# VectorE's share of a softmax: steps one by one with three buffers each, checks grouped by four sets, a plan priced by issue intervals, and 117 key tiles shared out by set

## The chip, the cores and the metric

The kernel runs on one core of a Trainium2 chip. The metric is the device time of one execution in microseconds (us). The engines are TensorE (PE in the profile, its weight loads PEld), VectorE (DVE), ScalarE (ACT), GpSimd (POOL) and SyncE (SP, here a queue that issues DMAs).

## The reference

Two attention layers on the same input x (2048 rows, 512 columns, bf16, 32 heads of 16), mixed by a gate g for each row:

```python
g = sigmoid((x * gate_w).sum(-1, keepdims=True))
# A: linear attention with a learned feature map
phi = concat([softmax(q_or_k @ w_phi), softmax(-(q_or_k @ w_phi))])   # 32 features a head
a = (phi_q @ (phi_k^T @ v)) / (phi_q @ phi_k.sum(rows) + 1e-6) @ A_wo
# B: ordinary attention
b = softmax(q @ k^T * 16**-0.5) @ v @ B_wo
out = g * a + (1 - g) * b
```

Layer B holds nearly all of the work: 32 heads x 2048 x 2048 scores, each of which needs an exponential.

## The kernel before, in words

**Sets and key tiles.** Layer B is cut into 32 sets. A set is one chunk of 512 queries (`qc`, four), one group of eight heads (`g`, four) and one half of that group (`par`, two): four heads. Each set goes over 16 key tiles (`kt`) of 128 keys. For a key tile and a set there are 4 heads x 512 queries of scores, made by TensorE (L745) in two pairs of 128x1024 scores, each in one of three slots of PSUM (`R_r`).

**Two ways to the exponential.** For most key tiles ScalarE takes the exponential of a pair from PSUM (L764, tile E in SBUF, a ring of eight buffers; the first ones lie in memory that layer A uses later, with the names phiK and vA). For `NDVE[n]` of the 16 key tiles of set n, 109 over all sets, VectorE makes the exponential from integer arithmetic: two conversions from PSUM to int16 (L754, named `di` in the plan) into a tile I, a mask step from I to F (L770, `dm`), a product of I and F into F (L773, `dw`), and a mask step on I (L777, `de`). All these tiles are named D in the profile. The products with the values are then made from F and from I (L787) where ScalarE's tiles need one such product (L800): four matmuls each, all added up in one PSUM bank, O, of which there is one. When a set's products are done, O is copied to SBUF (L464, tile OT), transposed (L825), divided by its sum (L829, L836), and its reciprocals go through a check on GpSimd (L831, L833, L835). The checks guard the shortcut without a maximum in the softmax: a verdict at the end (L899 to L904) would start a slow exact path, which doesn't run with these inputs.

**Wide packs.** `WIDE` is 2: VectorE's key tiles of a set are taken in packs of two where there are two, and L770 and L777 then take both in one instruction of 4096 elements. The memory for it is three wide tiles, two for I (`I_r`) and one for F (`F_r`).

**Projections and layer A.** In between run the projections of K and Q for the groups (L470; the copies L492 and L464), in one further PSUM bank (`M_r`), the projection of V, layer A's feature maps (ScalarE L627, VectorE L629 and L633, GpSimd's product L634) and its small products, and the output projection (L876, L884, L889, L892, DMAs at L894). A Q block, but for the first, is copied to `qs` and then spread over zeroed tiles `q` by eight DMAs on SP's queue (L514). The first one is masked by four VectorE steps instead (L505). GpSimd sets the other three q tiles to zero (L441).

**The order.** A planner in the kernel's own Python (`_Sched`) sets the order of each engine's instructions ahead of time. Every operation has a price in us, a due time (`prio`, mostly from `ut(u)`, where 32 units are one set) and buffers; the planner places operations one after the other by those prices. On the chip only the order is left: each engine goes through its list, and waits for semaphores where an operation needs another's result or buffer. `KLEAD`, `KLEAD1` and `QLEAD` say how many units ahead of its set a K or Q block is due, `RUSH_K` how many us earlier than due it may push in on TensorE, `LEAD` how far VectorE's tiles run ahead, `FULL` at how many occupied E buffers products that free one are put first, and `SLACK` and `LAT` are waits that the plan adds after an operation.

Of the kernel before, what the change touches and what calls it, by code (L numbers as in the profile page):

```python
# [7 lines left out]
F32 = mybir.dt.float32  # L8
# [26 lines left out]
NDVE = [0, 1] + [4, 3, 4, 4, 3] * 6  # L35
LEAD = 6.0
EXTRA = 1.2
WIDE = 2
FULL = 9
SLACK = 0.8  # L40

LAT = 0.06
STAY = 1.0
PAIRS = (0, 1, 2, 3, 4, 5, 6, 7)
RUSH = 1.0
# [3 lines left out]
RUSH_O = 30.0  # L49
VLEAD = 3.0  # L50
KLEAD1 = 24
KLEAD = 56
QLEAD = 24
EARLY = 10.0
# [23 lines left out]
class _Op:  # L78
    __slots__ = ("eng", "fn", "dur", "prio", "deps", "tiles", "mode", "name", "dma",
                 "n_open", "users", "after", "late", "start", "end", "count", "sem", "vc", "seq", "est", "parts", "feeds", "frees")  # L80


class _Sched:
# [9 lines left out]
    def add(self, eng, prio, dur, fn, deps=(), tiles=(), mode=None, name="", dma=None, nb=0.0, after=(), parts=1, feeds=None):  # L93
# [5 lines left out]
        o.mode, o.name, o.dma, o.est = mode, name, dma, nb  # L99
        o.frees = any(t.slots is self.stock for t in tiles)  # L100
# [8 lines left out]
    def next_pe(self, cands, first, last_mode):  # L109
# [5 lines left out]
        def rank(w, o):  # L115
            if o.feeds == "act" and pending("act", w) < (3 if last_mode == "row" else 2):
                return 0
            if short and o.frees:
                return 0.5
            if o.feeds == "dve" and pending("dve", w) < 1:  # L120
                return 1
            return 2
# [17 lines left out]
    def run(self):  # L140
# [16 lines left out]
        left = len(self.ops)  # L157

        def slot_time(t):
            best = None  # L160
            for i, ten in enumerate(t.slots.tenant):
                if ten is None:
                    when = 0.0
                elif any(x.end is None for x in ten.ops):
                    continue
                else:
                    when = max(x.end for x in ten.ops) + LAT
# [4 lines left out]
        def earliest(o, at):  # L172
            when = max(at, o.est)
            for t in o.tiles:
# [7 lines left out]
        while left:  # L182
# [16 lines left out]
            if pick is None:  # L199
                seen = set()  # L200
                for o in self.ops:
                    for t in o.tiles:
                        if id(t) not in seen and t.idx is not None and any(x.end is None for x in t.ops):
                            seen.add(id(t))
                            print("held", [(x.name, x.end, x.n_open) for x in t.ops][:8], str(t.slots.aps[0])[:60])
# [18 lines left out]
            o.end = w + dur + (o.dma or 0.0) + (0.17 if o.eng == "pe" else 0.0)  # L224
# [10 lines left out]
            for u in o.users:  # L235
                u.n_open -= 1
                late = u.late if o.end > 60 and u.eng == "pe" and o.eng in ("dve", "pool") else 0.0
                u.est = max(u.est, o.end + LAT + late)
# [85 lines left out]
def _build(ctx, nc, A_x, A_wqkv, A_w_phi, A_wo, B_wqkv, B_wo, gate_w, out):  # L324
# [39 lines left out]
    E_r = ring(8, [128, 1024], name="E")  # L364
    D_wide = [sb([128, 4096], I16, name="D")[:] for _ in range(3)]
    D_all = [d[:, 2048 * i:2048 * (i + 1)] for d in D_wide for i in range(2)]
    sch.stock = E_r
    I_r, F_r = _Slots(D_wide[0:2]), _Slots(D_wide[2:3])
    watv = WAT[:].rearrange("p a b -> p (a b)")
    eA_r = _Slots([watv[:, 1024 * i:1024 * (i + 1)] for i in range(4)])  # L370
    acc = sb([128, 136], F32, name="acc")
# [10 lines left out]
    rB_r = ring(3, [128, 4, 4], F32, name="rB")  # L382
# [15 lines left out]
    ez = acc[:, 80:96]  # L398
# [50 lines left out]
    MM = 0.235  # L449
    tset = [T0]  # L450
    for n in NDVE:
        tset.append(tset[-1] + 2 * (NT - n) * 0.935 + EXTRA)

# [7 lines left out]
    def evac(eng, prio, dst, src, deps, tiles, n=512, name="ev"):  # L461
        if eng == "act":
            return add("act", prio, 0.1 + n * 0.00084, lambda e: e.copy(dst(), src()), deps=deps, tiles=tiles, name=name)
        return add("dve", prio, 0.14 + n * 0.00105, lambda e: e.tensor_copy(dst(), src()), deps=deps, tiles=tiles, name=name)  # L464
# [18 lines left out]
    def k_proj(g, c, prio, tile, off, eng="dve"):  # L483
        f = fill(prio, tile, off, lambda t: W_Bk[:, t, 128 * g:128 * (g + 1)],
                 lambda t: xT[:, t, NQ * c:NQ * (c + 1)], op_x[c] + [op_wk1 if g else op_wk0], f"kf{g}{c}", RUSH_K)
        use_wk.append(f)
        dst, src = (lambda: kT[:, g, NQ * c:NQ * (c + 1)]), (lambda: tile.ap[:, off:off + 512])
        if eng == "act":
            ev_k[g, c] = add("act", prio, 0.53, lambda e: e.activation(dst(), src(), ACTF.Copy, scale=KFAC),
                             deps=[f], tiles=[tile], name=f"kev{g}{c}")  # L490
        else:
            ev_k[g, c] = add("dve", prio - RUSH_K, 0.68, lambda e: e.tensor_single_scalar(dst(), src(), KFAC, ALU.mult),  # L492
                             deps=[f], tiles=[tile], name=f"kev{g}{c}")

    def q_proj(g, c, prio, tile, off):

        f = fill(prio, tile, off, lambda t: W_Bq[:, t, 128 * g:128 * (g + 1)],
                 lambda t: xT[:, t, NQ * c:NQ * (c + 1)], op_x[c] + [op_wq1 if g else op_wq0], f"qf{g}{c}", RUSH_K)
        qt = q_t[g, c] = _Tile(q_r)
        if (g, c) == (0, 0):  # L500
# [7 lines left out]
            ev_q[g, c] = ms  # L508
            return
# [28 lines left out]
    for t in range(KT):  # L538

        def fn(e, t=t):  # L540
            ins = None
            for i in range(4):
                ins = e.transpose(txv()[:, t, 128 * i:128 * (i + 1)], xs[:, i, 128 * t:128 * (t + 1)], ident[:])
            return ins
        xtp.append(add("pe", -80 + t, 0.35, fn, deps=[op_x0, op_id], tiles=[tx], mode="full", name="xtp"))
    op_x[0] = [add("act", -80, 0.94, lambda e: e.copy(xT[:, 0:2, 0:NQ], txv()[:, 0:2, :]), deps=xtp[0:2], tiles=[tx], name="xev"),
               add("dve", -80, 0.69, lambda e: e.tensor_copy(xT[:, 2:4, 0:NQ], txv()[:, 2:4, :]), deps=xtp[2:4], tiles=[tx], name="xev")]  # L547
# [18 lines left out]
    for g in range(1, KT):  # L566
# [5 lines left out]
        q_proj(g, 0, ut(64 * g - QLEAD), t, 0)  # L572
# [8 lines left out]
    for part in range(4):  # L581
# [7 lines left out]
        gops.append(add("pe", ut(64), 0.5, gate_mm, deps=sum(op_x, []) + op_gw, tiles=[tg], mode="full", name="gate", nb=ut(60)))  # L589
# [8 lines left out]
    for w in range(2):  # L598
        for t in range(KT):
            tile = _Tile(M_r)  # L600
            prio = ut(66 + 4 * (4 * w + t))
# [7 lines left out]
            f = add("pe", prio, 0.35, fn, deps=[op_wat] + op_wbd, tiles=[tile], mode="full", name="wp", nb=prio - EARLY)  # L609
# [4 lines left out]
    accA, accB, okB, tmpB = acc[:, 0:64], acc[:, 64:80], acc[:, 96:112], acc[:, 112:128]  # L614
    op_acc0 = pool(-94.5, 0.2, lambda e: e.memset(acc[:, 0:80], 0.0), nb=LATER)
    op_acc = pool(-94.4, 0.2, lambda e: e.memset(acc[:, 96:112], 1.0), [op_acc0], nb=LATER)

    def phi(prio, w, st, dst, dst_deps, dst_tiles):
# [8 lines left out]
        o5 = [add("act", prio + 1, 0.58, lambda e, a=a: e.activation(ev()[:, :, a, :], P(), ACTF.Exp, scale=1.0 - 2.0 * a),  # L627
# [457 lines left out]
```

## Time and profile before

| | us |
|---|---|
| median of 3 runs (830.16 to 833.79) | 832.17 |
| the profiled execution, its own time | 833.28 |
| its span (first to last instruction) | 831.5 |
| ScalarE busy in the span | 782.4 (94%) |
| VectorE busy | 688.2 (83%) |
| TensorE busy, modelled ends | 745.2 (90%) |
| GpSimd busy | 149.3 (18%) |
| granted TensorE clock, mean | 0.982 |

In the lines of the profile a group is a source line, an engine and an operation with its tiles, then busy time and the mean of one in ns, then the idle time of the engine before them and what ended it. Durations on VectorE and ScalarE include the end of an instruction, over which the next one already starts: two that follow each other without a pause overlap by about 0.08 us on VectorE and 0.2 us on ScalarE. So the price of an instruction in a row of them is the time from its start to the next one's start, which the timeline shows. Windows give the busy time of each engine in a stretch of the span.

### The profile page before, as it was taken

To read this page: it belongs to the slowest core of one execution; us is meant where nothing else is said; L and a number is where in the kernel's file an instruction comes from. 1 tells how busy PE (TensorE), PEld (TensorE's weight loads), DVE (VectorE), ACT (ScalarE), POOL (GpSimd) and SP (SyncE) were. 2 spreads that over 40 slices of the span, in tenths; PEclk is the share of its full clock that TensorE was granted. 3 is DMA by queue.
4 is the path that set the end of the run, shared out by engine and by line. 5 is a ranking of instruction groups with operands and counts; after the bars stand their busy time and mean duration, and the time that the engine had idled before them with its cause. 6 is when DMAs were issued, how large, how long until landed. Compare 5 with 4: busy or idle time off the path is not lost.

```text
span 831.5 us, 13591 instructions
## 1 busy us (share of the span) xinstructions
PE 745.2 (90%) x5684; PEld 228.4 (27%) x5684; DVE 688.2 (83%) x747; ACT 782.4 (94%) x881; POOL 149.3 (18%) x195
## 2 busy tenths in 40 slices
PE   7999999989989999897798999989988999888886
PEld 2223232222222222232222222223222222222222
DVE  3255898889998999989989879899888988798891
ACT  3969999989999999999999899999999999899995
POOL 7000002212232323101032201120013111130000
PEclk9999999999999999999999999999999999899999
DMA  9100000100000000000202101111012110111000
GB/s 220 34 8 2 7 7 1 7 8 1 14 1 13 1 7 8 13 13 14 62 20 41 26 20 25 28 32 32 14 32 20 39 26 13 39 26 26 8 1 28
DMA packets 55922, 19.56 MB, mean 24 GB/s; under 512 B 48304, under 2 KB 55856, under 8 KB 55856
## 3 DMA queue, kind: packets, MB, share of 16 engines
q1 hardware_dynamic: 52960, 17.06, 9.6%
q10 hardware_dynamic: 2640, 1.57, 0.8%
q8 instruction: 46, 0.75, 0.4%
q14 instruction: 20, 0.16, 0.1%
q0 software_dynamic: 256, 0.02, 0.0%
HBM read 3.69 MB, written 2.10 MB: 7 GB/s over the span
## 4 chain that ended last, share of the span: by engine, by line
ACT 59%; PE 20%; DVE 17%; SPq 2%; issue 1%; DMA 1%; DVEq 0%
ACT E L764 54%; PE ps L745 8%; DVE D L754 4%; PE ps L470 4%; DVE D L773 4%; PE ps L800 3%; SPq L514 2%; DVE D L770 2%; ACT WAT L627 2%; PE ps L787 2%; ACT phiK L764 2%; PE ps L876 2%; DVE ss L629 2%; DVE D L777 1%; ACT vA L764 1%
## 5 line engine op out<-in xcount | busy, mean ns | idle before, releaser
L764 ACT ACTIVATE E<-ps 128x1024 bf16<-128x1024 f32 x782 | 728.9, 1144 | 27.1 <-PE ps L745 19.8
L745 PE MATMUL ps<-q,kT 64*128 64x512 bf16 x2048 | 372.8, 390 | 69.9 <-ACT E L764 43.0
L754 DVE TENSOR_SCALAR D<-ps 128x1024 int16<-128x1024 f32 x218 | 264.9, 1215 | 64.3 <-PE ps L745 63.6
L745 PEld LDWEIGHTS ps<-q,kT 64*128 64x128 bf16 x2048 | 92.0, 93 | 306.0 <-ACT E L764 217.7
L800 PE MATMUL ps<-E,vB 128*32 128x512 bf16 x1564 | 154.7, 396 | 2.3 <-ACT E L764 0.8
L773 DVE TENSOR_TENSOR D<-D 128x2048 bf16<-128x2048 bf16 x109 | 138.8, 1292 | 0.5
L787 PE MATMUL ps<-D,vB 128*32 128x512 bf16 x872 | 83.3, 398 | 0.6 <-DVE D L773 0.6
L770 DVE TENSOR_SCALAR D<-D 128x4096 int16<-128x4096 int16 (+1 forms) x61 | 70.3, 1153 | 7.1 <-PE ps L787 6.0
L777 DVE TENSOR_SCALAR D<-D 128x4096 int16<-128x4096 int16 (+1 forms) x61 | 73.5, 1205 | 0.2
L631 POOL TENSOR_TENSOR acc<-acc,ss 128x64 f32<-128x64 f32 x32 | 21.0, 656 | 286.3 <-DVE ss L629 286.3
L831 POOL TENSOR_TENSOR acc<-acc,rB 128x16 f32<-128x16 f32 x32 | 18.0, 563 | 289.5 <-DVE rB L829 289.5
L800 PEld LDWEIGHTS ps<-E,vB 128*32 128x32 bf16 x1564 | 38.6, 93 | 92.6 <-issue 79.9
L470 PE MATMUL ps<-Wp,xT 128*128 128x512 bf16 x128 | 49.7, 394 | 0.1
L470 PE MATMUL ps<-xT,WB 128*128 128x512 bf16 x128 | 48.1, 391 | 1.8 <-DVE xT L547 0.8
L629 DVE TENSOR_REDUCE ss<-WAT 128x64 f32<-128x1024 bf16 x32 | 38.8, 1211 | 2.1 <-ACT WAT L627 2.0
L634 POOL TENSOR_TENSOR WB<-WAT,ss 128x1024 bf16<-128x1024 bf16 x16 | 37.9, 2370 | 12.8 <-DVE ss L633 12.7
L627 ACT ACTIVATE WAT<-ps 128x512 bf16<-128x512 f32 x64 | 38.0, 701 | 0.8 <-PE ps L470 0.8
L634 POOL TENSOR_TENSOR phiK<-WAT,ss 128x1024 bf16<-128x1024 bf16 x16 | 34.6, 2163 | 16.7 <-DVE ss L633 16.7
L825 PE MATMUL ps<-ident,OT 128*128 128x128 f32 x128 | 33.9, 315 | 0.6 <-DVE Wp L892 0.3
L787 PEld LDWEIGHTS ps<-D,vB 128*32 128x32 bf16 x872 | 21.2, 95 | 38.0 <-issue 32.6
L876 PE MATMUL ps<-phiK 128*128 128x512 bf16 x88 | 30.4, 386 | 0.2 <-ACT E L764 0.2
L464 DVE CAST vB<-ps 128x1024 bf16<-128x1024 f32 x8 | 9.8, 1224 | 23.2 <-PE ps L470 23.2
(98 smaller groups left out, 375.8 us busy)
## 6 DMA issues: line engine op xcount, KB each, us to landing
out_dram<-Wp SPq DMA_DIRECT2D x16, 128.0 KB, 1.7
q<-qs SPq DMA_DIRECT2D x120, 16.0 KB, 1.8
WB<-in_B_wqkv_dram ACTq DMA_DIRECT2D x2, 384.0 KB, 11.0
D<-in_A_x_dram SPq DMA_DIRECT2D x1, 512.0 KB, 4.6
WB<-in_B_wqkv_dram ACTq DMA_DIRECT2D x1, 512.0 KB, 9.6
WAv<-in_A_wqkv_dram SPq DMA_DIRECT2D x1, 512.0 KB, 4.0
phiK<-in_A_wo_dram SPq DMA_DIRECT2D x1, 512.0 KB, 3.8
phiK<-in_B_wo_dram SPq DMA_DIRECT2D x1, 512.0 KB, 4.8
```

Of the source, the lines that this page charges most:

```text
L470: f = add("pe", prio - rush + 0.01 * t, MM, lambda e, t=t: e.matmul(tile.ap[:, off:off + 512], lhsT=lhs(t), rhs=rhs(t), start=(t == 0), st ...
L627: o5 = [add("act", prio + 1, 0.58, lambda e, a=a: e.activation(ev()[:, :, a, :], P(), ACTF.Exp, scale=1.0 - 2.0 * a), deps=[f], tiles=[til ...
L629: o6 = add("dve", prio + 5, 1.2, lambda e: e.tensor_reduce(ss.ap[:, 0, :], ee.ap.rearrange("p (g f) -> p g f", f=DH), AX.X, ALU.add), deps ...
L634: return add("pool", prio + 7, 2.0, lambda e: e.tensor_tensor(dst().rearrange("p (g f) -> p g f", f=DH), ee.ap.rearrange("p (g f) -> p g f ...
L745: ins = e.matmul(r.ap[:, 512 * i:512 * (i + 1)], lhsT=kT[p0:p0 + 64, g, 128 * kt:128 * (kt + 1)], rhs=qt.ap[p0:p0 + 64, 2 * pair + par, :] ...
L754: last_di = [add("dve", when - 6, 1.19, lambda e, r=r, I=I, part=part: e.tensor_scalar(I.ap[:, 1024 * part:1024 * (part + 1)], r.ap, EXP_B ...
L764: exps.append(add("act", when, 0.935, lambda e, r=r, E=E: e.activation(E.ap, r.ap, ACTF.Exp, scale=EXP_SCALE), deps=[q], tiles=[r, E], nam ...
L770: d1 = add("dve", pd, 0.15 + 0.55 * nk, lambda e, I=I, F=F, n=n: e.tensor_scalar(F.ap[:, 0:n], I.ap[:, 0:n], 0x007F, 0x3F00, op0=ALU.bitwi ...
L773: d4 = [add("dve", pd + 0.01 * y, 1.22, lambda e, I=I, F=F, lo=2048 * y: e.tensor_tensor(F.ap[:, lo:lo + 2048].bitcast(BF16), I.ap[:, lo:l ...
L777: d2 = add("dve", pd + 0.1, 0.15 + 0.55 * nk, lambda e, I=I, n=n: e.tensor_scalar(I.ap[:, 0:n], I.ap[:, 0:n], -128, 0x0001, op0=ALU.bitwis ...
L787: ins = e.matmul(O.ap[32 * s:32 * s + 32, :], lhsT=vB_[:, kt, VW * h:VW * h + 32], rhs=w.ap.bitcast(BF16)[:, base + 1024 * (s % 2) + 512 * ...
L800: ins = e.matmul(O.ap[32 * s:32 * s + 32, :], lhsT=vB_[:, kt, VW * h:VW * h + 32], rhs=es[s % 2].ap[:, 512 * (s // 2):512 * (s // 2 + 1)], ...
```

## The change

- **Shares.** 117 instead of 109 key tiles of VectorE, with a list for the 32 sets that is no longer periodic.
- **Steps one by one.** `WIDE` is 1: each key tile of VectorE has its own I and F, with mask steps of 2048 elements. The same memory is cut into three narrow tiles for I and three for F.
- **Checks.** The reciprocals of four sets are collected in one tile of 64 columns, and GpSimd's three check steps run once per four sets.
- **Plan.** Prices are set to other values (the exponential 0.904 instead of 0.935, VectorE's steps 1.133 instead of 1.19 to 1.22, and so on for nearly all operations); latencies differ by engine; GpSimd's operations and VectorE's mask and product steps are planned as sharing one port, so that the plan doesn't place them at the same time; leads and due times have other values.
- **Start.** GpSimd's zeroing of the three q tiles waits for the four mask steps of the first Q block.

```diff
-NDVE = [0, 1] + [4, 3, 4, 4, 3] * 6
-LEAD = 6.0
-EXTRA = 1.2
-WIDE = 2
-FULL = 9
-SLACK = 0.8
-
-LAT = 0.06
+NDVE = [1, 1, 4, 4, 4, 3, 4, 4, 3, 4, 3, 4, 4, 3, 5, 4, 4, 3, 4, 3, 5, 3, 4, 4, 5, 3, 4, 4, 4, 3, 5, 4]
+LEAD = 3.0
+EXTRA = 0.9
+WIDE = 1
+NI = 3
+NF = 3
+NE = 8
+FULL = 7
+FEW = 1
+SLACK = 0.6
+
+LAT = {"sp": 0.06, "act": 0.17, "pe": 0.2, "dve": 0.14, "pool": 0.24}
...
-RUSH = 1.0
+RUSH = 1.5
...
-RUSH_O = 30.0
+RUSH_O = 25.0
+RUSH_1 = 8.0
+QLEAD1 = 28
...
-KLEAD = 56
-QLEAD = 24
-EARLY = 10.0
+KLEAD = 40
+QLEAD = 32
+EARLY = 8.0
...
+        o.shared = eng == "pool" or name in ("dm", "de", "dw") or name.startswith("qm")
...
-            if o.feeds == "act" and pending("act", w) < (3 if last_mode == "row" else 2):
+            if o.feeds == "act" and pending("act", w) < (FEW if short else 3 if last_mode == "row" else 2):
                 return 0
             if short and o.frees:
                 return 0.5
-            if o.feeds == "dve" and pending("dve", w) < 1:
-                return 1
+            if o.feeds == "dve" and pending("dve", w) < (2 if short else 1):
+                return 0.4 if short else 1
...
+            if o.shared:
+                when = max(when, port["pool" if o.eng == "dve" else "dve"])
...
-    D_wide = [sb([128, 4096], I16, name="D")[:] for _ in range(3)]
-    D_all = [d[:, 2048 * i:2048 * (i + 1)] for d in D_wide for i in range(2)]
+    D_all = [sb([128, 2048], I16, name="D")[:] for _ in range(NI + NF)]
     sch.stock = E_r
-    I_r, F_r = _Slots(D_wide[0:2]), _Slots(D_wide[2:3])
+    I_r, F_r = _Slots(D_all[0:NI]), _Slots(D_all[NI:])
...
-                 lambda t: xT[:, t, NQ * c:NQ * (c + 1)], op_x[c] + [op_wk1 if g else op_wk0], f"kf{g}{c}", RUSH_K)
+                 lambda t: xT[:, t, NQ * c:NQ * (c + 1)], op_x[c] + [op_wk1 if g else op_wk0], f"kf{g}{c}", RUSH_K if g != 1 else RUSH_1)
...
+            for o in op_qz:
+                o.deps.extend(ms)
...
-        q_proj(g, 0, ut(64 * g - QLEAD), t, 0)
+        q_proj(g, 0, ut(64 * g - (QLEAD if g > 1 else QLEAD1)), t, 0)
...
-                            exps.append(add("act", when, 0.935, lambda e, r=r, E=E: e.activation(
+                            exps.append(add("act", when, 0.904, lambda e, r=r, E=E: e.activation(
...
-                        d1 = add("dve", pd, 0.15 + 0.55 * nk, lambda e, I=I, F=F, n=n: e.tensor_scalar(
+                        d1 = add("dve", pd, 0.06 + 0.54 * nk, lambda e, I=I, F=F, n=n: e.tensor_scalar(
...
-                        d4 = [add("dve", pd + 0.01 * y, 1.22, lambda e, I=I, F=F, lo=2048 * y: e.tensor_tensor(
+                        d4 = [add("dve", pd + 0.01 * y, 1.133, lambda e, I=I, F=F, lo=2048 * y: e.tensor_tensor(
...
+                if part == 3:
+                    rec = lambda rb=rb: rb.ap.rearrange("p a b -> p (a b)")
+                    c1 = add("pool", pr + 1, 0.4, lambda e, rec=rec: e.tensor_tensor(accB, accB, rec(), ALU.add),
+                             deps=recs + [op_acc] + chkB[-1:], tiles=[rb], name="chk")
+                    c2 = add("pool", pr + 1, 0.4, lambda e, rec=rec: e.tensor_single_scalar(rec(), rec(), 1.0 / BIG, ALU.is_ge),
+                             deps=reads + [c1], tiles=[rb], name="chk")
```

## The prediction

> **What bounds the kernel now.** I read the page first: busy shares, then the costliest groups.
>
> ```profile
> PE 745.2 (90%) x5684; PEld 228.4 (27%) x5684; DVE 688.2 (83%) x747; ACT 782.4 (94%) x881; POOL 149.3 (18%) x195
> L764 ACT ACTIVATE E<-ps 128x1024 bf16<-128x1024 f32 x782 | 728.9, 1144 | 27.1 <-PE ps L745 19.8
> L754 DVE TENSOR_SCALAR D<-ps 128x1024 int16<-128x1024 f32 x218 | 264.9, 1215 | 64.3 <-PE ps L745 63.6
> L773 DVE TENSOR_TENSOR D<-D 128x2048 bf16<-128x2048 bf16 x109 | 138.8, 1292 | 0.5
> ```
>
> ScalarE is the bound: busy 94%, and 59% of the chain that ended last. Durations of neighbours overlap, so the price of an instruction is its start-to-start time: the chain has 79 exponentials in 72.59 us, 0.919 each (0.904 where nothing disturbs them). VectorE is next at 83%. TensorE's 745 us are modelled ends; its queue spends 217.7 us waiting for exponentials, so it has room.
>
> An average hides stages, so next the windows (columns after the window: PE, weight loads, DVE, ACT, POOL, clock, DMA).
>
> ```profile
> 0.00:52.00 52.00, 44.52 (x234) 14.33 (x235) 16.71 (x17) 34.01 (x38) 15.89 (x34) 1.00 0.48 103
> 52.00:208.00 156.00, 145.06 (x1095) 44.45 (x1092) 129.97 (x142) 150.02 (x170) 21.06 (x28) 0.99 0.03 5
> 208.00:338.00 130.00, 119.94 (x857) 34.98 (x856) 121.92 (x130) 128.87 (x150) 38.72 (x38) 1.00 0.03 7
> 416.00:806.00 390.00, 352.80 (x2742) 107.62 (x2737) 341.61 (x373) 377.54 (x422) 64.39 (x80) 0.97 0.12 25
> ```
>
> From 208 to 338 us ScalarE is busy 99.1% while VectorE is busy 93.8%: both can run nearly full together. From 416 to 806 VectorE has only 87.6% and ScalarE 96.8%. The first 52 us leave ScalarE idle for 18. The timeline of ScalarE, VectorE and GpSimd there shows why:
>
> ```profile
> 15.34 1.02 ACT L764 ACTIVATE phiK<-ps 128x1024 bf16<-128x1024 f32 x1 [5.03 <-PE ps L745]
> 53.08 7.44 ACT L764 ACTIVATE E<-ps 128x1024 bf16<-128x1024 f32 x8 [6.48 <-PE ps L800]
> 10.65 4.85 DVE L505 TENSOR_SCALAR q<-q,masks 128x512 bf16<-128x512 bf16 x4
> 9.01 5.31 POOL L441 MEMSET q<- 128x2048 bf16 x3
> ```
>
> The four mask steps lie exactly beside GpSimd's zeroing of q, and the first exponential waits for them. Before 53.08 the eight E buffers are full and TensorE, without a pause since 39.65, has projections in front of the products that would free one.
>
> **The change, part by part.**
>
> *Exponentials.* 117 key tiles instead of 109 go to VectorE: 8 x 2 = 16 exponentials fewer, 16 x 0.919 = 14.7 us off ScalarE. By set: one tile in set 1, two in sets 3 to 16, five in sets 17 to 32.
>
> *VectorE's added work.* Start to start, undisturbed, in the trace: conversion (L754) 1.135, product (L773) 1.133, wide mask steps (L770, L777; 4096 elements) 1.132 each, narrow ones (2048) 0.609. A tile by single steps costs 2 x 1.135 + 1.133 + 2 x 0.609 = 4.62; eight: +37.0 us. Splitting the 48 wide pairs costs 48 x 2 x (2 x 0.609 - 1.132) = +8.3 us. The durations say the same less exactly:
>
> ```profile
> L777 DVE TENSOR_SCALAR D<-D 128x4096 int16<-128x4096 int16 x48 | 63.5, 1324 | 0.0
> L777 DVE TENSOR_SCALAR D<-D 128x2048 int16<-128x2048 int16 x13 | 10.0, 768 | 0.2
> ```
>
> [...]
>
> So VectorE gets +45.3 us against 688. Is there room? I counted the late window at undisturbed intervals: VectorE 319.4 us of work, ScalarE 369.5, in 390. After: VectorE 319.4 + 5 x 4.62 + 25 pairs (48 by the window's share of the time from 52 us on) x 0.172 = 346.8; ScalarE 369.5 - 10 x 0.904 = 360.5. At ScalarE's present rate (369.5/390) that takes 380.5 us and VectorE must run at 91%. By the same count single sets of before (between copies of O at L464) reach 0.90 and 0.97 together, as those ending at 332.9, 655.2 and 679.5; none holds more than 0.91. So the late stage is at the edge of what is seen: I take 3 us of the 14.7 as not realised, since the demand lies on the edge and not beyond it (bounds: 0, and 14 where VectorE is held to 88% as from 208 to 338 us: 346.8/0.88 = 394 instead of 380.5).
>
> *Buffers.* Two wide I and one wide F become three and three narrow ones, the same bytes. With one F, L770 waits for the products of the pack before:
>
> ```profile
> DVE D L770 <- PE ps L787: 6.0, 3, 5.0
> DVE D L754 <- PE ps L745: 63.6, 74, 3.3
> ```
>
> The 6.0 us go; the 63.6 is VectorE's reserve, which is what the 45.3 us use up. When it is gone, the next in line is the single O bank: a set's last products wait for VectorE's last tile, the copy of O behind them, and the next set's products behind that.
>
> *Checks.* 96 GpSimd steps of 16 columns become 24 of 64: 39.8 us of GpSimd become about 24 x 0.32 = 8. GpSimd has 18% load, so this counts only through VectorE. Undisturbed L773 takes 1.133 and beside GpSimd work 1.434 on average (28 cases); all such excess sums to 28 us, but 19 lie beside the phi products (L634), 3.6 beside the zeroing, only some 3 beside checks. I take 2 us of VectorE, off the path (bounds 0 and 3). At the end the checks run from 822.99 to 823.85 and their verdict at 825.3 lies before the last output step at 826.56: three steps of 0.32 instead of 0.22 to 0.25 add 0.3, hidden; without that cover it costs 0.3.
>
> [...]
>
> *Start.* The zeroing now waits for the mask steps. The trace does not show L505 undisturbed; the nearest row is a narrow L770 (2048 elements, 0.609), four times the size, so two steps on the path take 1.2 at most instead of 4.21. The slope of narrow to wide puts one at about 0.22, two at 0.43. The gain is 3.0 to 3.8, taken as 3.0, because the value projections then compete for TensorE. What is queued behind the zeroing (sums, masks, ones) is first used after 50 us, and the zeroed q at 54.
>
> The 6.48 stall: the group-1 projections are due 12 us later (RUSH_1 8, not 20), four K blocks and one Q block: 20 matmuls x 0.217 = 4.3 us that leave the crowded stretch, and products that free an E come earlier. The set's own value projections stay. I take 3 (0 to 6.5).
>
> *Later projections.* The Q block of group 3 (cast at 171.73, eight DMAs at 0.59 on SP's queue) lands at 178.58 and ScalarE idles 3.10 us. QLEAD 32 instead of 24 moves its cast about 6 us earlier. It goes; I take 2.5. Blocks of later query chunks keep their lead. K blocks of groups 2 and 3 come 16 units (half a set) later than now; no wait of before hangs on them, cost 0; if one came late, about 3, as the Q block.
>
> *Planning.* The plan's prices become 0.904, 1.133, 0.6, which are the trace's start-to-start times (before: 0.935, 1.19, 0.70). Only the engines' order comes of it. A truer order should save some of the 20 us that ScalarE idles in the middle; nothing here prices it. Bounds: 10 better, 15 worse; taken as 0. TensorE has 32 more product matmuls, 8 x 0.33 = 2.6 us under its waits; 2.6 if they were gone.
>
> **Sum.** Span 831.5 - 14.7 + 3 - 3.0 - 3 - 2.5 = 811.3. The profiled execution is 1.8 above its span (833.28) and the median of the runs 1.1 below that (832.17): 812.0 us.
>
> **Rivals.** "Within 0.5%" means 828.0 to 836.3, about what a measurement of this kernel can tell from no change.
>
> 1. *The order is better too* (12%): the late stage's stalls go as well. From 416 to 806, 390 - 369.5/0.97 = 9 us are lost against the good sets, and some startup idling beyond my terms: 800 us. For it: truer prices, separate F buffers. Against: half-clock spells of TensorE at 382, 416, 457, 522, 621 and 720 us, which no plan knows.
> 2. *The plan changes nothing, VectorE eats the late gain* (20%): late stage 390 as now, so of ScalarE's 14.7 only the early six exponentials (5.5) remain, and the start's 6; the Q block's 2.5 is lost elsewhere: 832.2 - 11.5 = 820.7. For it: 91% is the highest rate seen.
> 3. *VectorE becomes the bound and the kernel is slower* (18% by over 0.5%, 10% ends within it). Place: set ends from 416 us on, at the one O bank. With VectorE kept to 83% there (it runs at 82% now), 346.8/0.83 = 418, +28 - 11.5: 849. It decides from where the late stage eats 11.5, 402 us: VectorE below 86%. For it: in ten of the late sets VectorE is under 0.85 now, and its work arrives in lumps of 4.6 us. Against: there it idles for want of scores (63.6 us), not because it can't go faster; 208 to 338 shows 88% beside ScalarE's 97%.
>
> **How the numbers follow.** The forecast has 40% (803 to 818), rival 1 12%, rival 2 20%, rival 3 28%. Faster: 0.40 + 0.12 + 0.20 = 0.72; same 0.10; slower 0.18. The range 799 to 838 leaves out half of rival 1 and three quarters of the slower cases, 0.06 + 0.13. The faster cases' own range is 797 to 826.
>
> **What would show it.** Right: 790 exponentials in all, ScalarE busy near 768; VectorE near 730 and 93% or more from 416 us to the end stage; its wait for scores at L754 well under 63.6; four mask steps under 2.5 us together, the first exponential near 12; the stall at 46.6 halved; the one at 176 gone. Wrong: ScalarE's idle time from 416 on above 20 us, with TensorE waiting for L773 or for the copy of O; VectorE's steps not shorter beside GpSimd; or a new wait for K blocks of groups 2 and 3.

## The result, and the profile after

The changed kernel takes 790.7 us (790.62 to 795.78) where the kernel before takes 832.17: ratio 0.952, interval 0.9475 to 0.9561. The forecast was faster, 812.0, range 799 to 838. The direction held, the size didn't: 41.5 us instead of 20.2. One of the four runs took 795.78 us at a granted clock of 0.993, the other three 790.62 to 790.71 at 0.998 to 1.000.

The page after, section 1 and the groups that answer to those of before (the exponential is now L771, the scores L752, conversion L761, product L780, mask steps L777 and L784, products with the values L807 and L794):

```profile
PE 708.3 (90%) x5645; PEld 224.7 (28%) x5716; DVE 710.5 (90%) x883; ACT 764.3 (97%) x865; POOL 121.1 (15%) x123
L771 ACT ACTIVATE E<-ps 128x1024 bf16<-128x1024 f32 x766 | 713.2, 1185 | 4.3 <-PE ps L807 2.2
L761 DVE TENSOR_SCALAR D<-ps 128x1024 int16<-128x1024 f32 x234 | 284.5, 1216 | 21.7 <-PE ps L752 21.1
L780 DVE TENSOR_TENSOR D<-D 128x2048 bf16<-128x2048 bf16 x117 | 141.4, 1209 | 0.6
L784 DVE TENSOR_SCALAR D<-D 128x2048 int16<-128x2048 int16 x117 | 81.7, 698 | 0.1
```

ScalarE waits 4.3 us before its exponentials instead of 27.1, VectorE 21.7 instead of 64.3 before its conversions. By the waits nearly all of the latter are still waits for scores, and the wait of the first mask step for products (6.0 before) no longer stands among the long ones:

```profile
DVE D L761 <- PE ps L752: 21.1, 39, 1.2
```

The chain that ended last is ScalarE's to 87% (59% before). The same windows (the last one ends where the span's tail begins, 764 instead of 806):

```profile
0.00:52.00 52.00, 45.88 (x264) 14.68 (x272) 19.99 (x24) 38.12 (x43) 15.62 (x34) 1.00 0.43 102
52.00:208.00 156.00, 144.20 (x1137) 45.31 (x1148) 141.12 (x173) 156.00 (x178) 20.32 (x16) 1.00 0.03 6
208.00:338.00 130.00, 119.24 (x939) 38.20 (x950) 123.62 (x153) 129.90 (x152) 32.76 (x23) 1.00 0.03 6
416.00:764.00 348.00, 313.48 (x2586) 98.40 (x2614) 337.90 (x424) 347.28 (x391) 39.31 (x36) 1.00 0.13 25
```

From 416 to 764 us ScalarE is busy 99.8% and VectorE 97.1% at once, and TensorE's granted clock is 1.00. From 52 to 764 us ScalarE has 710.46 of 712 us; before it had 731.53 of the 754 from 52 to 806. So the span's 42.7 us divide as follows: ScalarE's busy time 18.1 less (782.4 to 764.3), its idle time in the first 52 us 4.1 less (18.0 to 13.9), in the middle 20.9 less (22.5 to 1.5), at the end 0.4 more. Two remarks on this division. The stall of 6.48 us before ended at 53.08, so 1.1 of the 20.9 belong to the start. And of the 18.1, the 16 exponentials make up 14.7: with them back (e3 below) ScalarE is busy 779.0. I put the other 3.4 down to fewer pauses, as an instruction in front of a pause counts with its whole end: an exponential there lasts 1.05 us in the trace of before (median of 39) and takes 0.904 in a row, and ScalarE's instructions are followed by a pause 46 times before and 20 times after (an estimate: 26 x 0.146 = 3.8).

The start, by the timeline of ScalarE, VectorE and GpSimd:

```profile
11.55 1.02 ACT L771 ACTIVATE phiK<-ps 128x1024 bf16<-128x1024 f32 x1 [1.99 <-PE ps L752]
47.02 1.02 ACT L771 ACTIVATE E<-ps 128x1024 bf16<-128x1024 f32 x1 [1.36 <-PE ps L807]
9.90 0.88 DVE L510 TENSOR_SCALAR q<-q,masks 128x512 bf16<-128x512 bf16 x3
12.77 5.29 POOL L446 MEMSET q<- 128x2048 bf16 x3 [3.75 <-DVE q L510]
```

Three mask steps take 0.88 us with GpSimd out of the way; the zeroing waits for them. The first exponential comes 3.8 us earlier: 3.0 from the wait in front of it (5.03 to 1.99), the rest from ahead of the masks, where the traces differ anyway (ScalarE's first copy of K starts between 8.96 and 10.05 us over all runs of this case, 9.71 before and 8.96 here). The stall of 6.48 is now 2.8 us in four pieces.

### The profile page after: what moved, and what is told of

It is laid out like the page before. It is cut to its first block, busy times and chain, and to the rows that moved or that the text cites. A ratio compares the mean times of both kernels' runs of the same rounds, so it can differ in the third digit from the quotient of the medians.

```text
span 788.8 us, 13621 instructions
## 1 busy us (share of the span) xinstructions
PE 708.3 (90%) x5645; PEld 224.7 (28%) x5716; DVE 710.5 (90%) x883; ACT 764.3 (97%) x865; POOL 121.1 (15%) x123
## 4 chain that ended last, share of the span: by engine, by line
ACT 87%; PE 6%; DVE 4%; DMA 2%; SPq 1%; issue 0%
ACT E L771 80%; ACT WAT L634 4%; PE ps L752 2%; ACT phiK L771 2%; PE ps L475 1%; DVE D L761 1%; DMA xT<-in_A_x_dram 1%; ACT vA L771 1%; PE ps L891 1%; PE ps L807 1%; SPq L521 1%; DVE D L777 1%; DVE D L780 1%; SPq L409 1%; PE ps L665 0%; DMA WB<-WB 0%
## 5 line engine op out<-in xcount | busy, mean ns | idle before, releaser
L771 ACT ACTIVATE E<-ps 128x1024 bf16<-128x1024 f32 x766 | 713.2, 1185 | 4.3 <-PE ps L807 2.2
L752 PE MATMUL ps<-q,kT 64*128 64x512 bf16 x2048 | 362.8, 385 | 58.1 <-ACT E L771 45.7
L761 DVE TENSOR_SCALAR D<-ps 128x1024 int16<-128x1024 f32 x234 | 284.5, 1216 | 21.7 <-PE ps L752 21.1
L752 PEld LDWEIGHTS ps<-q,kT 64*128 64x128 bf16 x2048 | 89.8, 93 | 275.2 <-ACT E L771 214.3
L807 PE MATMUL ps<-E,vB 128*32 128x512 bf16 x1532 | 149.1, 389 | 5.0 <-issue 4.3
L780 DVE TENSOR_TENSOR D<-D 128x2048 bf16<-128x2048 bf16 x117 | 141.4, 1209 | 0.6
L794 PE MATMUL ps<-D,vB 128*32 128x512 bf16 x936 | 90.8, 386 | 1.6 <-issue 1.0
L777 DVE TENSOR_SCALAR D<-D 128x2048 int16<-128x2048 int16 x117 | 83.8, 717 | 1.1
L784 DVE TENSOR_SCALAR D<-D 128x2048 int16<-128x2048 int16 x117 | 81.7, 698 | 0.1
L807 PEld LDWEIGHTS ps<-E,vB 128*32 128x32 bf16 x1532 | 37.8, 93 | 85.4 <-issue 77.5
L475 PE MATMUL ps<-xT,WB 128*128 128x512 bf16 x111 | 40.2, 388 | 3.3 <-ACT WAT L634 1.4
L475 PE MATMUL ps<-Wp,xT 128*128 128x512 bf16 x98 | 38.0, 389 | 0.5 <-DVE OT L469 0.3
L641 POOL TENSOR_TENSOR phiK<-WAT,ss 128x1024 bf16<-128x1024 bf16 x16 | 35.6, 2222 | 10.7 <-DVE ss L640 10.7
L641 POOL TENSOR_TENSOR WB<-WAT,ss 128x1024 bf16<-128x1024 bf16 x16 | 33.5, 2096 | 14.3 <-DVE ss L640 14.3
L794 PEld LDWEIGHTS ps<-D,vB 128*32 128x32 bf16 x936 | 23.7, 94 | 37.5 <-issue 29.0
L835 PE MATMUL ps<-ident,OT 128*128 128x128 f32 x128 | 27.6, 300 | 0.5 <-ACT WAT L634 0.3
L848 POOL TENSOR_TENSOR acc<-acc,rB 128x64 f32<-128x64 f32 x8 | 5.1, 633 | 133.9 <-DVE rB L840 133.9
```

The source lines that it names most:

```text
L475: f = add("pe", prio - rush + 0.01 * t, MM, lambda e, t=t: e.matmul(tile.ap[:, off:off + 512], lhsT=lhs(t), rhs=rhs(t), start=(t == 0), st ...
L641: return add("pool", prio + 7, 1.95, lambda e: e.tensor_tensor(dst().rearrange("p (g f) -> p g f", f=DH), ee.ap.rearrange("p (g f) -> p g ...
L752: ins = e.matmul(r.ap[:, 512 * i:512 * (i + 1)], lhsT=kT[p0:p0 + 64, g, 128 * kt:128 * (kt + 1)], rhs=qt.ap[p0:p0 + 64, 2 * pair + par, :] ...
L761: last_di = [add("dve", when - 6, 1.133, lambda e, r=r, I=I, part=part: e.tensor_scalar(I.ap[:, 1024 * part:1024 * (part + 1)], r.ap, EXP_ ...
L771: exps.append(add("act", when, 0.904, lambda e, r=r, E=E: e.activation(E.ap, r.ap, ACTF.Exp, scale=EXP_SCALE), deps=[q], tiles=[r, E], nam ...
L777: d1 = add("dve", pd, 0.06 + 0.54 * nk, lambda e, I=I, F=F, n=n: e.tensor_scalar(F.ap[:, 0:n], I.ap[:, 0:n], 0x007F, 0x3F00, op0=ALU.bitwi ...
```

## The experiments

Three questions: what the shares are worth, which part of the plan removed the 20.9 us, and whether it is the plan's truth (its numbers are the chip's) or the picking of one lucky set of values. Ratios are to the kernel before, run beside them (its median there was 829.4 to 831.3); "+" is the distance from the changed kernel's 790.7, whose own ratio is 0.9475 to 0.9561.

| kernel | us | ratio (95%) | + |
|---|---|---|---|
| e1 before, Q blocks due earlier | 825.95 | 0.996 (0.9939 to 0.9972) | |
| e2 before, 117 tiles | 844.43 | 1.017 (1.0128 to 1.0211) | |
| e5 before, new prices, latencies, port | 820.05 | 0.987 (0.9831 to 0.9905) | |
| e18 after, checks each set | 795.89 | 0.956 (0.954 to 0.9587) | 5.2 |
| e13 after, VectorE's prices +1% | 796.33 | 0.959 (0.9555 to 0.9623) | 5.6 |
| e14 after, LEAD 3.2 | 799.02 | 0.962 (0.9586 to 0.9654) | 8.3 |
| e17 after, old start | 799.59 | 0.961 (0.9589 to 0.9638) | 8.9 |
| e15 after, all prices +5% | 802.62 | 0.965 (0.9617 to 0.9691) | 11.9 |
| e3 after, 109 tiles | 803.97 | 0.969 (0.9648 to 0.9722) | 13.3 |
| e9 after, old leads and rules | 804.19 | 0.969 (0.9666 to 0.9717) | 13.5 |
| e16 after, 121 tiles | 805.7 | 0.971 (0.9666 to 0.9743) | 15.0 |
| e12 after, VectorE's prices -8% | 809.12 | 0.975 (0.9729 to 0.9779) | 18.4 |
| e6 after, old latencies | 809.41 | 0.975 (0.9688 to 0.9807) | 18.7 |
| e11 after, no port in the plan | 811.3 | 0.979 (0.9752 to 0.9825) | 20.6 |
| e8 after, TensorE's old prices | 816.9 | 0.983 (0.9794 to 0.9868) | 26.2 |
| e10 after, wide packs | 817.89 | 0.985 (0.9826 to 0.9877) | 27.2 |
| e4 after, all old prices, latencies, no port | 830.75 | 1.002 (0.9995 to 1.0039) | 40.1 |
| e7 after, VectorE's old prices | 840.15 | 1.011 (1.0069 to 1.0158) | 49.5 |

The expectations stand with each run. Seven runs lie outside every range that they name: e1, e4, e5, e7, e9, e12 and e13.

### Were the late Q blocks the cause? (e1)

```diff
-QLEAD = 24
+QLEAD = 32
...
-            q_proj(g, c, ut(64 * (4 * c + g) - 44), t, 0)
+            q_proj(g, c, ut(64 * (4 * c + g) - 64), t, 0)
```

> The kernel before with one edit: Q blocks are due earlier (those of later query chunks 64 units ahead of their set instead of 44, those of the first chunk 32 instead of 24). Theory A, the idle time in the middle came from Q blocks that landed late, each followed by a half-clock spell of TensorE: before, ScalarE's gaps at 176, 415, 520, 622 and 720 us and in the half-clock spells behind them sum to 12 us, so 820 to 823 us. Theory B, the truer prices of the plan removed the idle time, the Q blocks being one symptom of an order that runs behind: 829 to 834, with new stalls elsewhere.

In the profile before, TensorE waited four times for a late block; three of these gaps (those that end at 415, 621 and 720 us) had a half-clock spell of TensorE behind them, the one that ends at 179 had none, and the stall at 520, which the expectation counts among them, followed by the waits a step of layer A on VectorE (L688). One block, by the timelines of TensorE and ScalarE before:

```profile
720.25 0.61 PE L745 MATMUL ps<-q,kT 64*128 64x512 bf16 x2 [2.17 <-DMA q<-qs]
721.85 1.02 ACT L764 ACTIVATE E<-ps 128x1024 bf16<-128x1024 f32 x1 [2.10 <-PE ps L745]
724.85 1.02 ACT L764 ACTIVATE E<-ps 128x1024 bf16<-128x1024 f32 x1 [0.49 <-PE ps L745]
```

With earlier blocks these stalls after 400 us and their spells are gone (no half-clock spell between 245 us and the tail), yet only some 4 us are gained (0.4%), a third of what theory A expects. Other waits take their place: ScalarE waits 12.2 us for products that free an E buffer, 6.3 of them after the start, where the kernel before has 0.2. So the late blocks were a part of the idle time, not its cause as a whole; that they are a symptom of an order that runs late is a reading that fits and that this run alone doesn't show.

### What are the shares worth? (e2, e3, e16)

```diff
-NDVE = [0, 1] + [4, 3, 4, 4, 3] * 6
+NDVE = [1, 1, 4, 4, 4, 3, 4, 4, 3, 4, 3, 4, 4, 3, 5, 4, 4, 3, 4, 3, 5, 3, 4, 4, 5, 3, 4, 4, 4, 3, 5, 4]
```

This is e2, alone on the kernel before; e3 is its undoing on the changed kernel; e16 has 4 instead of 3 in sets 6, 11, 18 and 26 on the changed kernel.

> The kernel before with the new list of 117 key tiles alone, all else old (wide packs, old prices, old leads). If the shares alone carry a good part of the gain: 14.7 us less, 817 to 819. If VectorE in the old order can't take them (rivals 2 and 3 of the prediction): 822 to 850, with ScalarE idle over 60 us and TensorE waiting for the O copy or L773.

> The changed kernel with the old list of 109 key tiles. If ScalarE alone is the bound of the changed kernel, its 16 more exponentials cost 16 x 0.919 = 14.7: 804 to 807, ScalarE still above 96% busy. If VectorE at 97% holds it back too, the tiles given back relieve VectorE and the cost is smaller: 796 to 801.

> The changed kernel with four tiles more on VectorE (121, in sets 6, 11, 18 and 26 by one more). ScalarE's work falls by 8 x 0.919 = 7.4, VectorE's rises by 18.5. VectorE is busy 96 to 97% from 78 us on, so it is the bound now: 798 to 815, with ScalarE idle. If VectorE still had room: 784 to 788, and then it beats both kernels.

In the old order the eight tiles cost 14 us; in the new one they bring 13.3. e3 is nearly the price of ScalarE's 16 exponentials (14.7): ScalarE is the bound of the changed kernel. e2 is the third rival: ScalarE's work fell, and its wait for products, shown here by the waits of e2, rose from 6.7 us to

```profile
ACT E L764 <- PE ps L800: 34.2, 18, 6.9
```

With the four tiles more of e16 ScalarE has 8 exponentials fewer and the kernel is 15 us slower. VectorE's busy share from 78 us on rises only from 96.6% (to 764) to 97.3% (to 770), and ScalarE waits for products. The plan's values were not set anew for 121 tiles, and a step off them costs 6 to 8 us by itself (e13, e14 below), so this shows an edge of this plan more than one of the engines. By the waits of e16:

```profile
ACT E L771 <- PE ps L807: 18.4, 9, 6.7
```

### Which part of the plan? (e4 to e8, e11)

The edits, in order: e4 puts back all prices, e6 the latencies, e7 and e8 one engine's prices, e11 takes the shared port out of the plan, e5 puts prices, latencies and port into the kernel before. The lines that weigh most:

```diff
# e6 (also in e4)
-LAT = {"sp": 0.06, "act": 0.17, "pe": 0.2, "dve": 0.14, "pool": 0.24}
+LAT = {"sp": 0.06, "act": 0.06, "pe": 0.23, "dve": 0.06, "pool": 0.06}
# e7 (also in e4): VectorE's prices, as
-last_di = [add("dve", when - 6, 1.133, ...
+last_di = [add("dve", when - 6, 1.19, ...
-d4 = [add("dve", pd + 0.01 * y, 1.133, ...
+d4 = [add("dve", pd + 0.01 * y, 1.22, ...
# e8 (also in e4): TensorE's prices, as
-n2.append(add("pe", pr, 0.165, ...
+n2.append(add("pe", pr, 0.3, ...
# e11 (also in e4)
-o.shared = eng == "pool" or name in ("dm", "de", "dw") or name.startswith("qm")
+o.shared = False
```

> The changed kernel planned with the prices and latencies of before and without the shared port in the plan; structure, shares and leads stay new. Theory B (prices): most of the 21 us of idle time in the middle return, 807 to 815, with half-clock spells. Theory A (late Q blocks, cured by leads): 791 to 796, no more than one or two half-clock spells.

> The kernel before (109 tiles, wide packs, old leads, checks for every set) planned with the new prices and latencies and the shared port. If the prices alone make the good order: the idle time in the middle falls from 22 us to 5, 808 to 814. If they need the new structure or leads to work: 822 to 836.

> The changed kernel with the old latencies alone in the plan (0.06 us after every operation, 0.17 more after TensorE's, where the change has 0.14 after VectorE's, 0.17 after ScalarE's and 0.24 after GpSimd's); prices and port new. If the latencies make the order, since with them too small every hand-over between engines comes later than planned: 808 to 825. If the durations make it: 791 to 797.

> The changed kernel with VectorE's old prices alone (conversion 1.19 instead of 1.133, product 1.22 instead of 1.133, mask steps 0.70 instead of 0.60, copies 0.68 instead of 0.60). A planned tile of VectorE is then 5.0 instead of 4.6 us, 8% too dear, so the plan believes VectorE late and places its scores late. If VectorE's share of the prices carries the gain: 810 to 830. If not: 791 to 798.

> The changed kernel with TensorE's old prices alone (transposes 0.30 instead of 0.165, layer A's products 1.2 and 0.5 to 0.6 instead of 0.5 and 0.2 to 0.25, projections 0.235 instead of 0.217). TensorE waits for ScalarE for over 200 us in the trace, so its prices should matter little: 791 to 798. If TensorE's order is what they spoil: 803 to 820.

> The changed kernel planned without the shared port of GpSimd and VectorE; all else new. In the changed kernel VectorE's mask steps still lie beside the phi product for some 7 us in all. If the port in the plan only shifts this: 791 to 796. If it carries weight, as an unplanned 1 to 2 us at a VectorE that runs at 97% makes a set end late: 798 to 812.

e4 settles the main question: with shares, buffers, checks, start and leads all new and only the plan's numbers old, nothing of the gain is left (1.002). ScalarE is busy 768.3 us of 827.4, so the exponentials are saved and the time goes into 59.1 us of idling (49.1 before). Theory A, leads alone, falls; theory B holds, and its 807 to 815 was too mild. How much of this is the harm of 117 tiles under the old numbers (e2, e7) isn't separated: no run has the new structure with 109 tiles and the old numbers. The converse, e5, brings 11 us: the new numbers need something of the rest (shares, buffers, checks, start, leads) for more, and e10 and e9 below say that buffers and leads are among it. The steps don't add up: put back one by one they cost far more than 41.5 together.

The latencies alone are 18.7 (e6). My expectation that TensorE's prices matter little was wrong (26 us): it waits for ScalarE over 200 us, and yet with its old prices ScalarE waits for it. By the waits of e8, where the changed kernel has 2.0 and 2.2:

```profile
ACT E L771 <- PE ps L752: 13.4, 19, 1.6
ACT E L771 <- PE ps L807: 10.2, 4, 4.4
```

My reading is that what the plan puts in front of a score on TensorE delays an exponential.

e7 shows how a wrong price turns into time. With a VectorE tile planned at 5.0 us, 0.4 more than it takes, 117 tiles give VectorE about as much work in the plan as ScalarE (an estimate: 710.5 + 117 x 0.4 = 757 us of busy time against 764.3), and its tiles pile up at set ends. On the chip it runs like this (timelines of VectorE, TensorE and ScalarE of e7, one set end):

```profile
654.68 1.23 DVE L761 TENSOR_SCALAR D<-ps 128x1024 int16<-128x1024 f32 x1 [1.14 <-PE ps L752]
656.42 1.22 DVE L761 TENSOR_SCALAR D<-ps 128x1024 int16<-128x1024 f32 x1
657.56 1.22 DVE L780 TENSOR_TENSOR D<-D 128x2048 bf16<-128x2048 bf16 x1
657.70 0.59 PE L752 MATMUL ps<-q,kT 64*128 64x512 bf16 x2 [1.34 <-DVE D L761]
658.83 0.62 PE L794 MATMUL ps<-D,vB 128*32 128x512 bf16 x4 [0.54 <-DVE D L780]
659.89 1.22 DVE L780 TENSOR_TENSOR D<-D 128x2048 bf16<-128x2048 bf16 x1
661.03 1.22 DVE L761 TENSOR_SCALAR D<-ps 128x1024 int16<-128x1024 f32 x1
662.95 1.23 DVE L761 TENSOR_SCALAR D<-ps 128x1024 int16<-128x1024 f32 x1
664.75 0.68 DVE L469 COPY OT<-ps 128x512 f32<-128x512 f32 x1
665.49 1.90 PE L807 MATMUL ps<-E,vB 128*32 128x512 bf16 x16 [0.22 <-DVE OT L469]
666.16 1.02 ACT L771 ACTIVATE E<-ps 128x1024 bf16<-128x1024 f32 x1 [11.26 <-PE ps L807]
```

Read from below: an exponential waits 11.26 us for an E buffer; the products that free one wait for the copy of O; the copy for VectorE's last tiles of the set and its place in VectorE's queue; and VectorE works them off from 654.68 to the copy with one pause of 0.11 us. TensorE waits for VectorE there, so its half-clock spell at this place (13.7 us from 657.8) isn't what holds the set end up.

e11 shows what the shared port in the plan is worth. In the changed kernel VectorE's mask steps L777 and L784 lie beside the phi product (L641) in 14 cases and lose some 7 us there; without the port in the plan product and mask steps do so in 24 cases and lose some 24. VectorE's busy time says the same: 729.5 us in e11, 710.5 in the changed kernel. In the trace of the changed kernel L777 lasts 0.69 us away from GpSimd (median of 106) and 1.24 on average in the seven cases beside the phi product, the longest, at 386.13 us, 2.42. By what mechanism the one delays the other, the runs don't show; the shared port is the plan's assumption.

### Buffers and leads (e10, e9)

```diff
# e10
-WIDE = 1
+WIDE = 2
...
-    D_all = [sb([128, 2048], I16, name="D")[:] for _ in range(NI + NF)]
+    D_wide = [sb([128, 4096], I16, name="D")[:] for _ in range(3)]
+    D_all = [d[:, 2048 * i:2048 * (i + 1)] for d in D_wide for i in range(2)]
-    I_r, F_r = _Slots(D_all[0:NI]), _Slots(D_all[NI:])
+    I_r, F_r = _Slots(D_wide[0:2]), _Slots(D_wide[2:3])
# e9: LEAD 6, EXTRA 1.2, SLACK 0.8, RUSH 1, RUSH_O 30, RUSH_1 20, QLEAD1 24, QLEAD 24, KLEAD 56, EARLY 10, FULL 9, old ranks
```

> The changed kernel with wide packs of two tiles, two wide I and one wide F as before; prices, leads and shares new. VectorE's work falls by some 54 pairs x 0.172 = 9 us. If VectorE's work is what counts: 786 to 791. If the finer steps with three buffers each are what lets VectorE run at 97%: 800 to 825, with L770's counterpart waiting for products and ScalarE for E buffers at set ends.

> The changed kernel with all old leads, due times and ranking rules of the planner (LEAD 6, EXTRA 1.2, SLACK 0.8, RUSH 1, RUSH_O 30, RUSH_1 20, QLEAD 24, QLEAD1 24, KLEAD 56, EARLY 10, FULL 9, the old ranks); prices, buffers and shares new. If true prices are enough: 791 to 800, with Q-block stalls back at most. If the leads carry as much as the prices: 808 to 830.

By the prices wide packs save VectorE some 9 us. Its busy time doesn't show that (710.6 us, 710.5 in the changed kernel), and the kernel is 27 us slower. By the groups of e10 ScalarE waits 23.9 us before its exponentials, nearly as long as in the kernel before, but mostly for products, where before 19.8 of 27.1 were for scores:

```profile
L772 ACT ACTIVATE E<-ps 128x1024 bf16<-128x1024 f32 x766 | 714.2, 1167 | 23.9 <-PE ps L808 15.4 <-PE ps L753 8.2
```

The sign that I expected for the single F, a mask step that waits for products, isn't there: the first mask step's wait is 1.4 us in all. Whether the size of the step or the single F does it, this run doesn't separate. The old leads cost 13.5 us, between the two expectations: they carry weight, but less than the prices.

### Truth or picking? (e12 to e15)

```diff
# e12 (and e13: 1.1443 and 0.6060)
-last_di = [add("dve", when - 6, 1.133, ...
+last_di = [add("dve", when - 6, 1.0424, ...
-d1 = add("dve", pd, 0.06 + 0.54 * nk, ...
+d1 = add("dve", pd, 0.5520 * nk, ...
# e14
-LEAD = 3.0
+LEAD = 3.2
# e15: every price times 1.05, as
-exps.append(add("act", when, 0.904, ...
+exps.append(add("act", when, 0.9492, ...
```

> The changed kernel with the prices of VectorE's four steps 8% too low in the plan (1.042 and 0.552 instead of 1.133 and 0.60), the mirror of the old ones. Theory C, the plan must be true: too cheap is as bad as too dear, 810 to 840. Theory D, too dear prices hurt only because 117 tiles then fill the plan's VectorE beyond its ScalarE: too cheap ones leave it room, 791 to 802.

> The changed kernel with the prices of VectorE's four steps 1% too high. The trace's own times differ from the plan's by as much (ScalarE's exponential is planned at 0.904 and takes 0.911 on average). Theory C, true prices are what counts: 790 to 795. Theory E, the exact choice of values was picked among many near ones and any step off it costs some 10 us: 798 to 815.

> The changed kernel with LEAD 3.2 instead of 3.0: all prices true, VectorE's tiles due 0.2 us earlier, which changes the order at many places and no quantity. Theory C: 790 to 796. Theory E: 798 to 815.

> The changed kernel with all prices and latencies of the plan 5% too high, so that their ratios stay true. If the ratio between the engines is what counts: 790 to 798. If each error counts, as leads and DMA times stay as they are: 800 to 815.

Both hold in part, and the runs don't part them cleanly. A step that is no truer or falser than the change's own choice costs 5.6 and 8.3 us (e13, e14): so much seems to come from this set of values being a particularly good one. (For e13 and e18 even that is near the noise: their intervals overlap with the changed kernel's, of whose four runs one took as long.) Steps that leave all prices true can cost more, 13.5 (e9) and 15.0 (e16), so the 11.9 of e15 doesn't show by itself that an untrue plan is worse. Above these lie the false numbers: 18.4 (e12), 18.7 (e6), 20.6 (e11), 26.2 (e8) and 49.5 (e7). And the true numbers alone gain 11 us in the kernel before (e5), whose other values are the old ones. So I take the plan's truth as the larger part and the picking as a smaller one; a search for good values around the old numbers, which would settle it, was not run.

Too cheap is bad (18.4), so theory D isn't the whole; but too dear is worse (49.5), as its mechanism, VectorE overfull in the plan, would have it. The two steps are no exact mirror, since e7 also raises VectorE's copies and smaller steps. That an error in the ratio between the engines is worse than one in all prices isn't shown: 5% on all cost 11.9, 8% off VectorE's four steps 18.4.

### Start and checks (e17, e18)

```diff
# e17
-            for o in op_qz:
-                o.deps.extend(ms)
-RUSH_1 = 8.0
-QLEAD1 = 28
+RUSH_1 = 20.0
+QLEAD1 = 24
# e18
-                if part == 3:
-                    rec = lambda rb=rb: rb.ap.rearrange("p a b -> p (a b)")
+                rec = lambda rb=rb, part=part: rb.ap[:, part, :]
...
```

> The changed kernel with the old start: the zeroing of q doesn't wait for the mask steps, RUSH_1 20 and QLEAD1 24. The prediction's terms for the start are 3.0 and 3.0 us. The step also changes the order in the first sets, which e13 and e14 price at 6 to 8 us in the worst case: 793 to 800. The first exponential should come near 14 us instead of 11.5, and the stall before 55 us be 3 to 6 us longer.

> The changed kernel with the reciprocals checked after each set again (96 GpSimd steps of 16 columns, planned at 0.3 each with the shared port), all else new. The prediction's term for the checks was 2 us of VectorE's time, off the path. VectorE now runs at 97%, so each us beside it counts, and the planned port moves its mask steps about: 793 to 805. If checks cost nothing but the step off the chosen order: 796 to 800.

By e17's timeline of ScalarE the start is as before:

```profile
15.38 1.02 ACT L769 ACTIVATE phiK<-ps 128x1024 bf16<-128x1024 f32 x1 [5.12 <-PE ps L750]
51.73 1.02 ACT L769 ACTIVATE E<-ps 128x1024 bf16<-128x1024 f32 x1 [3.31 <-PE ps L805]
```

ScalarE is busy 37.42 of the first 56 us there, which take in the whole stall, and 42.12 in the changed kernel: the start is worth 4.7 us, the rest of e17's 8.9 is no more than a step off the chosen order. e18's 5.2 is no more than such a step either; GpSimd's busy time rises from 121.1 to 150.8 and VectorE's stays (710.7 against 710.5).

No kernel here beats the changed one.

## Why the prediction was wrong

**Exponentials: right in the new order.** 790 of them; e3 puts the eight tiles at 13.3 us against 14.7 less 3. Under the old plan numbers nothing is left of them (e2, e4).

**VectorE's room: wrong.** The step "none holds more than 0.91", and so "the late stage is at the edge of what is seen: I take 3 us", read the rate of before as a ceiling. It was a demand: VectorE idled for want of scores. Counted at undisturbed intervals, VectorE's rate from 416 to 728 us is now 0.93 or more, its busy share 97%, and ScalarE loses nothing. With this plan's values 121 tiles are beyond the edge (e16).

**VectorE's work: sized too high.** Busy near 730 was expected, 710.5 measured. The narrow mask steps cost 0.60, near the 0.609 taken, and the steps of the tiles at undisturbed intervals rose by 42.5 us, near the 45.3. What fell is the time lost beside GpSimd: 18.4 us beside the phi products and 3.6 beside the zeroing before, some 7 now, where I had 2 for the checks and nothing for the shared port in the plan; and with fewer pauses fewer ends of instructions count as busy (VectorE's instructions are followed by a pause 204 times before and 151 times after; two without a pause overlap by 0.083). (The prediction's 28 us of excess is about VectorE's whole busy time less its work at undisturbed intervals, 688.2 less 659.7 by a recount, so it holds such ends too and not only GpSimd's part.)

**Planning: the step that failed.** The prediction says of a truer order "nothing here prices it. Bounds: 10 better, 15 worse; taken as 0." It is the largest term of all: ScalarE's idle time in the middle fell by 20.9 us, of which 1.1 belong to the start's stall and 3.1 to the Q block of group 3, so that some 17 had no term. And e4 is the changed kernel with this term at 0: the sum has 812 for it, it takes 830.75. So the forecast's "faster" came true through the term that it left out, which is luck: without it the other terms, 20 us of gain on paper, come to nothing. The term could have been bounded from the profile: the idle time of the bounding engine was 22.5 us from 52 to 806, about 18 without those two pieces, and that, not 10, was the end of the range. I set part of it aside as "half-clock spells ... which no plan knows". They changed with the order: there is none in the middle of the changed kernel, and e4 has four between 52 us and its tail.

**Later Q blocks: wrong.** "Blocks of later query chunks keep their lead" in units, yet their stalls are gone too; e1 shows that moving the blocks alone gains a third of the 12 us. The block of group 3 went as forecast: 3.1 us of stall at 179, 2.5 taken, and no pause there now.

**Start: right.** The wait for the masks shrank by 3.0 us (3.0 taken) and the stall by 3.7 (3 taken); a wait of 1.83 us for the transposed x is new (its DMA lands at 14.45 in the chain of the changed kernel). Up to 56 us ScalarE idles 13.9 us instead of 19.1: 5.2 of the 6 us. One reading was off without effect: TensorE had a pause of 0.62 us at 50 us, in what the prediction calls a stretch without one.

**Rivals.** The first, a better order, is what happened; its 800 was too weak by 9 us, for the same reason as the sum. The third is true of the shares without the plan: e2 is 1.7% slower, and e7 shows its mechanism at its place, the one O bank. I had tied it to VectorE's rate, but the same VectorE works at 97% in the changed kernel; what e7 changes is the order alone.

## What to carry to other kernels

Where a fixed order feeds several engines, the idle time of the bounding engine in the middle of the span is about the bound on what a better order can win there, and here nearly all of it was won (20.9 of 22.5 us); price that before calling it unpriced. A planner's prices should be start-to-start times from a trace, with the hand-over between engines in it (e6, 18.7 us) and with what VectorE loses beside GpSimd (e11, 20.6 us): putting one group of them back cost 19 to 50 us here. Whether work moved to a second engine pays hangs on the order: the same eight tiles were worth +14 us in one plan and -13 us in the other.

## What the runs showed of the hardware

In these runs half-clock spells of TensorE often followed short pauses. In the profile before, spells of 3.4 us (once 6.8) at a granted clock of 0.5 began at 382, 416, 522, 621 and 720 us, 0.9 to 2.9 us after the beginning of TensorE pauses of 1.3 to 2.2 us; four pauses of 1.3 to 1.6 us, at 10, 13, 177 and 637, brought none, and two spells (85 and 457) came without a pause over 0.9. Over all traces of this case, from 20 us to 30 us before the end, 12 of 13 recorded pauses of 1.89 us or more had a spell within 3.5 us of their beginning, but only 7 of 27 from 1.2 to 1.6 us. What decides whether a pause brings one, these traces don't show.

VectorE and ScalarE were busy 97.1% and 99.8% for 348 us together (416 to 764 us of the changed kernel), beside a TensorE that fed both and was busy 313.48 us of them by its modelled ends.
